# Token groups of an attention and two-MoE kernel: 512, 512, 512 and 768 tokens instead of 512, 512, 640 and 640

## The chip, the core and the metric

The kernel runs on one core of one Trainium2 chip. The metric is the device time of one execution in microseconds (us). The time before is 1117.15 us, the median of three runs (1117.76, 1117.15 and 1112.87).

## The reference

Four batches of 576 tokens, eight heads of 64 columns. Decayed causal attention gives 2304 rows of 512 columns, then come an RMS norm and two gated feed-forward layers, all in float32:

```python
def _moe_ref(x, w_gate, w_val, w_out, rms_g):
    rms = np.sqrt(np.mean(x * x, axis=-1, keepdims=True) + 1e-06)
    xn = x / rms * rms_g
    g = xn @ w_gate
    silu = g * (1.0 / (1.0 + np.exp(-g)))
    val = xn @ w_val
    return (silu * val @ w_out).astype(np.float32)
```

The second layer does the same without the norm. `w_gate` and `w_val` are 512 x 1536, `w_out` is 1536 x 512.

## The kernel before

**Groups.** Each batch's 576 tokens are cut into a block of 256 and a block of 320 (`QN`, L32). The four groups (`GROUPS`, L37) are the 256-blocks of batches 0 and 1, those of 2 and 3, the 320-blocks of 0 and 1, and the 320-blocks of 2 and 3. So the feed-forward layers run over 512, 512, 640 and 640 tokens. The attention of group g+1 runs in between the matmuls of group g: `attention` (L1481) starts each pair of heads when group g has done a given number of its 72 steps a layer pair (`steps`, `UNIT_SPREAD` L59; the last two entries belong to the last group).

**Matmuls.** A float32 operand is split into a high part in a 32-bit matmul format and the rest, and each product is three matmuls: high x high, high x low, low x high (`mm3`, L1668). Activations lie with the model dimension on the partitions, so a matmul's moving operand has as many columns as tokens. Weights come in 36 pieces of 128 x 512 a layer: 24 for gate and value, 12 for the output. A piece takes part in four tiles of 128 x 128, so a group of one matmul width has 2 layers x 36 pieces x 4 tiles x 3 = 864 matmuls. `moe` (L1682) goes over the groups. In groups 0 and 1 one thread works on both blocks at once, 512 columns a matmul. In group 2 the two blocks do not fit in 512, so two threads (`thread` 0 and 1) each do 320 columns with the same piece: 1728 matmuls of 320. Of these a third are output products, with `H` (and `late_h`) as moving operand; the rest have `X`.

**The last group** uses a seven-product scheme (`seven` L1371, `seven_out` L1261): a 2 x 2 block product with 7 instead of 8 products, its two column halves being the two 320-blocks. It has 1512 matmuls of 320 columns (L1388 to L1390 and L1306 to L1308). `right` (L1054) makes its moving operands (`b11`, `b21`, `b22`, `t1` to `t4`, for two row halves: 14 splits into high and low) from the normed attention output `xT`. `make_sums` (L1109) makes its weight sums ahead of time, during groups 1 and 2, paced by `S_AT` (L53): two pieces loaded, two results stored, for 36 units. `left` (L1148) and `out_left` (L1177) load them.

**Buffers.** Weight pieces live in eight 512 KB slots (`whl`), with three more (`XW`) once the attention is over; `XT32` adds five float32 load buffers, and `STS` five tiles for partial sums.

**Order.** All instructions are ordered at build time by a planner (`Plan`, L127): it gives each engine a cost function for each operation, lets generators wait for events and buffer slots, and issues what can start first. `either` picks among engines, with a handicap such as `HAND_LO`. All DMAs go out on one queue, SP, in the planned order. What the chip executes is this fixed order on each engine, with semaphores.

**Norm.** `norm` (L945) waits for a block's eight heads, sums squares, and scales. For groups 0 to 2 it writes a temporary that `split_x` (L1029) splits into `X`; for the last group it scales `xT` in place (L1011), and `right` takes it from there, block by block.

Of the kernel before, what the change touches and what calls it, by code (L numbers as in the profile page):

```python
# [8 lines left out]
F32 = mybir.dt.float32  # L9
# [21 lines left out]

QN = (SPLIT, S - SPLIT)  # L32
# [3 lines left out]
NMAX = max(QN)  # L36
GROUPS = ((0, (0, 1)), (0, (2, 3)), (1, (0, 1)), (1, (2, 3)))  # L37
# [16 lines left out]
XW, XT32, BSLOTS, STS = 3, 5, 3, 5  # L54
# [4 lines left out]
UNIT_SPREAD = ((0, 0), (0, 0), (-16, 1), (12, 5), (4, 4), (36, 4), (4, 4), (28, 4))  # L59
# [4 lines left out]
HAND_T = 0.0  # L64
HAND_CONV = (0, 0, 0, 0, 0)
# [192 lines left out]
def tile_attention_moe_moe(  # L258
# [76 lines left out]
    mb_slots = Slots(tiles(MB, [P, NMAX], F32, "mb"))  # L335
# [17 lines left out]
    zeros = HH[MT - 1][1][:, 1]  # L353
# [17 lines left out]
    rows = late_h.rearrange("p m i s n -> p (m i s n)")  # L371
    lent = [rows[:, 2 * i * WP : 2 * (i + 1) * WP].rearrange("p (t w) -> p t w", t=2) for i in range(LENT)]
# [95 lines left out]
    tt_here, out_p7, h_free, HQ = Event(), Event(), (Event(), Event()), []  # L468
# [7 lines left out]
    TT["t1"] = [[x[:, 1, :NMAX] for x in XX[c]] for c in range(2)]  # L476
# [154 lines left out]
    def pair_queries(hds, before, started, done):  # L631
# [97 lines left out]
        e = yield hi_op(n, xT[h // 2][s][:, :n], bank[:, :n], e, xT_free[hd.g][s], psum=True)  # L729
# [185 lines left out]
    def wide_values(hd, x, hl, ready, used_, done):  # L915
# [6 lines left out]
        def mm():  # L922
# [12 lines left out]
        to = xT[k][s][r0 : r0 + D, :n]  # L935
# [3 lines left out]
            "DVE", dve(n), lambda: nc.vector.tensor_tensor(to, bank[:D, :n], o[:D, :n], op=ALU.add), e, xT_free[hd.g][s]  # L939
# [5 lines left out]
    def norm(g, s, done):  # L945
# [3 lines left out]
        for k in range(KT):  # L949
            both = (done[2 * k], done[2 * k + 1])  # L950
            x = xT[k][s]
            if k == 0:
                e = yield op("ACT", act(n), lambda: nc.scalar.activation(acc[:, :n], x[:, :n], AF.Square), *both)
            else:
                sq, e0 = yield Take(tmp_slots, both)
                e1 = yield op("ACT", act(n), lambda: nc.scalar.activation(sq[:, :n], x[:, :n], AF.Square), e0, *both)
# [191 lines left out]
    def left(i):  # L1148
# [9 lines left out]
        for x, n, src, ready in (  # L1158
# [12 lines left out]
            spawn(load_split(n, t, o, src, ready, es[x], e0, e1), pr)  # L1171
# [37 lines left out]
    def load_split(n, t, o, src, ready, ev, *deps):  # L1209
# [7 lines left out]
        e = yield lo_op(n, lo, t[:, :n], hi, e, *deps)  # L1217
# [3 lines left out]
    def finish_pair(layer, m, s, bank, e, half, mid):  # L1221

        n = NMAX
        yield wait(mid, e, *h_free)
# [7 lines left out]
            "DVE", dve(n), lambda: nc.vector.tensor_tensor(o, th[:, :n], bank[:, :n], op=ALU.mult), e, mid, *h_free,  # L1232
# [28 lines left out]
    def seven_out(layer, g, at0):  # L1261

        n = NMAX
# [28 lines left out]
        for q, (p, x, off, name) in enumerate(OUT):  # L1292
# [30 lines left out]
            progress(g, at0, 0)  # L1323

    def combine(layer, d, bank, made):
        n = NMAX

        def out_(dd, s, b, a, *deps):
            if not layer:
                e = yield op("DVE", dve(n), lambda: nc.vector.tensor_tensor(xT[dd][s][:, :n], b[:, :n], a, op=ALU.add), *deps)  # L1330
# [4 lines left out]
            spawn(send(dd, s, z, e), 0.1)  # L1335
# [28 lines left out]
    def send(d, s, z, e):  # L1364
        kind, blocks = GROUPS[NG - 1]
        n = QN[kind]
        rows = out[d * P : (d + 1) * P].rearrange("p (b t) -> p b t", b=B)[:, blocks[s], QOFF[kind] : QOFF[kind] + n]
        e = yield op("SP", dma(P * 4 * n), lambda: nc.sync.dma_start(rows, z[:, :n]), e)
        tmp_slots.give(z, e)

    def seven(layer, base, m):  # L1371

        n = NMAX
# [4 lines left out]
        def rights(name):  # L1378
# [3 lines left out]
            return [[x[:, s, :n] for x in XX[k + c]] for c in range(2)]  # L1382
# [140 lines left out]
    def switch():  # L1523
# [375 lines left out]
```

## Time and profile before

| | us |
|---|---|
| runs | 1117.76, 1117.15, 1112.87 |
| median | 1117.15 |
| profiled execution, its own time | 1114.52 |
| its span, first to last instruction | 1112.7 |
| busy: TensorE matmuls / VectorE / ScalarE / GpSimd | 1092.0 / 808.4 / 631.0 / 474.5 |
| group 0 and 1, matmuls of 512 columns | 69.3 to 562.4 |
| group 2, matmuls of 320 columns, two threads | 562.5 to 886.3 |
| last group, seven products | 886.4 to 1109.3 |

PE is TensorE, DVE VectorE, ACT ScalarE, POOL GpSimd, SP the queue that issues DMAs. A matmul's listed duration is longer than its share of the engine, because matmuls overlap; the cost of one in a dense stretch is the distance between the starts of two neighbours. The two rows of a matmul line that differ only in columns are different forms. The share of the DMA engines is a mean over 16; it can read a little over 1.

### The profile page before, as it was taken

How to read it: one execution, taken by the hardware profiler on the slowest of the kernel's cores; microseconds unless marked ns; L12 is line 12 of the kernel's file. 1: busy time of each engine (PE TensorE's matmuls, PEld its weight loads, DVE VectorE, ACT ScalarE, POOL GpSimd, SP SyncE). 2: the span in 40 equal slices, each digit the busy share in tenths (PEclk: the TensorE clock that was granted, in tenths of full speed). 3: DMA queues.
4: the chain of work that ended last, by engine and by line, in shares of the span. 5: the costliest groups of instructions: out<-in, count | busy, mean ns of one | idle time of the engine just before them, and what ended most of it. 6: DMA issues, size and time to landing. Idle time of an engine off the chain costs nothing.

```text
span 1112.7 us, 19530 instructions
## 1 busy us (share of the span) xinstructions
PE 1092.0 (98%) x6411; PEld 999.2 (90%) x6411; DVE 808.4 (73%) x1774; ACT 631.0 (57%) x1462; POOL 474.5 (43%) x502
## 2 busy tenths in 40 slices
PE   8989999998999999999999999999999999999998
PEld 7968888886888888888899999999999999999998
DVE  6988888888557757667567766676766278878884
ACT  5967788886556655766434554455553343453442
POOL 1323202224156566656354555364455564124410
PEclk8999999998999999999999999999999999999999
DMA  7655788675999775875989798786778656975694
GB/s 223 218 181 191 252 274 298 220 227 161 332 378 325 244 244 205 280 247 200 317 277 354 267 319 309 267 270 235 253 268 291 214 196 216 295 266 190 206 300 139
DMA packets 135225, 282.35 MB, mean 254 GB/s; under 512 B 13906, under 2 KB 56210, under 8 KB 135122
## 3 DMA queue, kind: packets, MB, share of 16 engines
q1 hardware_dynamic: 135124, 281.10, 74.5%
q8 instruction: 51, 0.84, 0.3%
q14 instruction: 50, 0.41, 0.1%
HBM read 194.32 MB, written 86.65 MB: 253 GB/s over the span
## 4 chain that ended last, share of the span: by engine, by line
PE 83%; DVE 7%; DMA 6%; POOL 2%; issue 2%; SPq 1%; ACT 1%; POOLq 0%; ACTq 0%
PE bank L1671 17%; PE bank L1673 17%; PE bank L1672 17%; PE bank L1389 4%; PE bank L1390 4%; PE bank L1388 4%; PE bank L926 3%; PE bank L898 3%; DMA w<-w_f 2%; PE bank L1308 2%; PE bank L1307 2%; PE bank L1306 2%; PE bank L789 2%; PE bank L790 2%; DMA w<-w 1%
## 5 line engine op out<-in xcount | busy, mean ns | idle before, releaser
L1671 PE MATMUL bank<-X,whl 128*128 128x320 f32 (+1 forms) x756 | 270.7, 358 | 3.3 <-ACT X L287 3.3
L1672 PE MATMUL bank<-X,whl 128*128 128x320 f32 (+1 forms) x756 | 264.4, 350 | 0.8 <-POOL X L292 0.6
L1673 PE MATMUL bank<-X,whl 128*128 128x320 f32 (+1 forms) x756 | 264.4, 350 | 0.0
L292 POOL TENSOR_TENSOR whl<-w,whl 128x512 fp32r<-128x512 f32 x123 | 159.5, 1300 | 185.4 <-ACT whl L287 128.8
L1671 PEld LDWEIGHTS bank<-X,whl 128*128 128x128 f32 x756 | 142.4, 188 | 17.4 <-ACT X L287 3.6
L1673 PEld LDWEIGHTS bank<-X,whl 128*128 128x128 f32 x756 | 142.2, 188 | 15.1
L1672 PEld LDWEIGHTS bank<-X,whl 128*128 128x128 f32 x756 | 142.6, 189 | 14.5 <-POOL X L292 1.1
L287 ACT CAST whl<-w 128x512 fp32r<-128x512 f32 x169 | 104.3, 622 | 70.2 <-DMA w<-w_sums 24.4
L1671 PE MATMUL bank<-H,whl 128*128 128x512 f32 (+1 forms) x272 | 98.6, 362 | 4.4 <-ACT whl L287 4.4
L1673 PE MATMUL bank<-H,whl 128*128 128x512 f32 (+1 forms) x272 | 96.9, 356 | 0.2 <-DVE whl L292 0.2
L1672 PE MATMUL bank<-H,whl 128*128 128x512 f32 (+1 forms) x272 | 96.7, 355 | 0.0
L1775 ACT ACTIVATE tmp<-bank 128x512 f32<-128x512 f32 (+1 forms) x96 | 50.0, 521 | 56.2 <-PE bank L1673 56.0
L1778 DVE SCALAR_TENSOR_TENSOR tmp<-tmp,bank 128x512 f32<-128x512 f32 (+1 forms) x96 | 55.9, 583 | 31.3 <-ACT tmp L1775 31.0
L1800 DVE SCALAR_TENSOR_TENSOR bank<-tmp,bank 128x320 f32<-128x320 f32 (+1 forms) x84 | 48.7, 580 | 33.5 <-PE bank L1673 32.7
L1607 POOL TENSOR_SCALAR w<-w,rebase 128x512 f32<-128x512 f32 x24 | 24.2, 1010 | 105.5 <-DVE wk L1619 42.0
L807 DVE TENSOR_REDUCE tm<-bank 128x1 f32<-128x512 f32 (+1 forms) x96 | 51.1, 561 | 17.7 <-PE bank L796 12.3
L1671 PEld LDWEIGHTS bank<-H,whl 128*128 128x128 f32 x272 | 51.3, 188 | 10.9 <-ACT whl L287 4.9
L1613 ACT ACTIVATE w<-w,kbias 128x512 uint8<-128x512 uint8 x41 | 60.1, 1465 | 1.0 <-DVE w L1605 0.6
L1673 PEld LDWEIGHTS bank<-H,whl 128*128 128x128 f32 x272 | 51.2, 188 | 7.3 <-DVE whl L292 0.9
L1672 PEld LDWEIGHTS bank<-H,whl 128*128 128x128 f32 x272 | 51.3, 189 | 5.6
L1805 ACT CAST H<-bank 128x320 fp32r<-128x320 f32 (+1 forms) x64 | 32.0, 500 | 41.0 <-DVE bank L1800 39.9
L910 DVE TENSOR_TENSOR pl<-bank,ph 128x512 fp32r<-128x512 f32 (+1 forms) x80 | 49.7, 631 | 6.7 <-ACT ph L287 6.1
(267 smaller groups left out, 2925.2 us busy)
## 6 DMA issues: line engine op xcount, KB each, us to landing
whl<-w_split SPq DMA_DIRECT2D x85, 512.0 KB
w<-w SPq DMA_DIRECT2D x72, 512.0 KB
w<-w_f SPq DMA_DIRECT2D x144, 256.0 KB
w_split<-whl SPq DMA_DIRECT2D x72, 512.0 KB
w_f<-w SPq DMA_DIRECT2D x72, 256.0 KB
w_sums<-w SPq DMA_DIRECT2D x48, 256.0 KB
w_sums_split<-whl SPq DMA_DIRECT2D x23, 512.0 KB
raw<-qk SPq DMA_DIRECT2D x32, 288.0 KB
```

The costliest lines, as they stand in the source:

```text
L287: nc.scalar.copy(o, i)
L292: (nc.vector if e == "DVE" else nc.gpsimd).tensor_tensor(o, a, b, op=ALU.subtract)
L807: em = yield op("DVE", dve(m), lambda: nc.vector.tensor_reduce(st[:, c + i : c + i + 1], bank[:, :m], axis=AX.X, op=ALU.max), e)
L910: e = yield op("DVE", dve(n), lambda: nc.vector.tensor_tensor(low, src, o.bitcast(F32), op=ALU.subtract), e)
L1388: nc.tensor.matmul(o, w[:, 0, cs], xh, start=c == 0, stop=False)
L1613: lambda e: nc.scalar.activation(u8[:, :, 4], u8[:, :, 3], AF.Identity, scale=1.0 / 32, bias=kbias)
L1671: nc.tensor.matmul(o, wh[:, cs], xh, start=start, stop=False)
L1672: nc.tensor.matmul(o, wh[:, cs], xl, start=False, stop=False)
L1673: nc.tensor.matmul(o, wl[:, cs], xh, start=False, stop=stop)
L1775: e = yield op("ACT", actp(n), lambda: nc.scalar.activation(th[:, :n], bank[:, :n], AF.Tanh, scale=0.5), e, e0)
L1778: lambda: nc.vector.scalar_tensor_tensor(th[:, :n], th[:, :n], 1.0, bank[:, :n], op0=ALU.add, op1=ALU.mult), e,
L1800: lambda: nc.vector.scalar_tensor_tensor(o, th[:, :w], factor, bank[:, :w], op0=ALU.mult, op1=ALU.mult), e, mid,
```

## The change

The groups of tokens become 512, 512, 512 and 768. Group 2 takes the whole 320-block of batch 0 and the first 192 tokens of batch 1's; the last 128 tokens of batch 1's block are normed in place in `xT` and join the last group, whose halves are now 384 columns (`NL`). `moe` has one thread; every matmul of groups 0 to 2 has 512 columns (`NW`) and every one of the last group 384. `xT`, `X` and `H` lose their block dimension and become plain rows of columns. `join` lets the last group's operand preparation wait for both blocks' norms. Output tiles go out in one DMA per run of tokens (`tokens`). In the last group there is one extra float32 load buffer instead of five and two extra weight slots instead of three; four of the five partial-sum tiles are the norm's old tiles. The heads' pace (`UNIT_SPREAD`), a priority for the last group's first weights (`HEAD_PRIO`) and two engine handicaps (`HAND_LAST`) change. What the attention computes is the same, and so are all weights that are loaded. The diff, cut to its core:

```diff
+NW, NL = 512, 384
+COLS = ((0, 256), (0, 256), (128, 448), (0, 320))
+LEFT_OVER = COLS[2][0] + NW
+TOKENS = (
+    ((0, 0, 256), (1, 0, 256)),
+    ((2, 0, 256), (3, 0, 256)),
+    ((0, 256, 320), (1, 256, 192)),
+    ((2, 256, 320), (3, 256, 320), (1, 448, 128)),
+)
...
-XW, XT32, BSLOTS, STS = 3, 5, 3, 5
+XW, XT32, BSLOTS, STS = 2, 1, 3, 1
...
-UNIT_SPREAD = ((0, 0), (0, 0), (-16, 1), (12, 5), (4, 4), (36, 4), (4, 4), (28, 4))
+UNIT_SPREAD = ((0, 0), (0, 0), (-16, 1), (12, 5), (4, 4), (32, 4), (4, 3.5), (28, 3.5))
...
+HEAD_PRIO = 1.2
+HAND_LAST = (0.2, 0.2)
...
-    def lo_op(n, o, i, hi, *deps):
-        hand = HAND_LO[plan.phase]
+    def lo_op(n, o, i, hi, *deps, hand=None):
+        hand = HAND_LO[plan.phase] if hand is None else hand
...
-    mb_slots = Slots(tiles(MB, [P, NMAX], F32, "mb"))
+    mbs, accs = tiles(MB, [P, NL], F32, "mb"), tiles(2, [P, NL], F32, "acc")
...
-    accs = tiles(2, [P, NMAX], F32, "acc")
-    xT = [tiles(2, [P, NMAX], F32, f"xT{k}_") for k in range(KT)]
...
-    XX = [tiles(2, [P, 2, NMAX], F32R, f"X{k}_") for k in range(KT)]
-    HH = [tiles(2, [P, 2, NMAX], F32R, f"H{m}_", hp) for m in range(MT - 3)]
-
-    late_h = hp.tile([P, 3, 2, 2, NMAX], F32R, name="late_h")
...
+    xT = tiles(KT, [P, 2 * NL], F32, "xT")
+    XX = [tiles(2, [P, 2 * NL], F32R, f"X{k}_") for k in range(KT)]
+    HH = [tiles(2, [P, NW], F32R, f"H{m}_", hp) for m in range(MT - 3)]
+    late_h = hp.tile([P, 3, 2, NW], F32R, name="late_h")
     HH += [[late_h[:, m, i] for i in range(2)] for m in range(3)]
...
-    def view(t, s, n):
-        return t[:, :, :n] if s is None else t[:, s, :n]
-
-    def part(t, s, n):
-        return t[:, :n] if s is not None else t[:, : 2 * n].rearrange("p (s n) -> p s n", s=2)
+    def cols(t, g, s):
+        c = COLS[g][s]
+        return t[:, c : c + QN[GROUPS[g][0]]]
...
-        if g == NG - 1:
-            for k in range(KT):
-                x = xT[k][s][:, :n]
-                e = yield op(
-                    "DVL", dve(n),
-                    lambda: nc.vector.scalar_tensor_tensor(x, x, gam[:, k : k + 1], rb[:, :n], op0=ALU.mult, op1=ALU.mult),
-                    eb, gam_here,
-                )
-                later(last_x[0][k][s], e)
-            mb_slots.give(rb, e)
-            return
-        for k in range(KT):
-            xn, e0 = yield Take(tmp_slots, (x_free[g][s], gam_here))
+
+        at = n if g < NG - 2 else QN[1] - (COLS[2][1] + QN[1] - LEFT_OVER) * s if g == NG - 2 else 0
+        for k in range(KT if at else 0):
+            xn, e0 = yield Take(tmp_slots, (x_free[g], gam_here))
             e = yield op(
-                "DVL", dve(n),
+                "DVL", dve(at),
                 lambda: nc.vector.scalar_tensor_tensor(
-                    xn[:, :n], xT[k][s][:, :n], gam[:, k : k + 1], rb[:, :n], op0=ALU.mult, op1=ALU.mult
+                    xn[:, :at], cols(xT[k], g, s)[:, :at], gam[:, k : k + 1], rb[:, :at], op0=ALU.mult, op1=ALU.mult
                 ), eb, e0,
             )
-            spawn(split_x(g, s, k, xn, e), 1)
+            spawn(split_x(g, s, k, xn, at, e), 1)
+        for k in range(KT if at < n else 0):
+            x = cols(xT[k], g, s)[:, at:]
+            e = yield op(
+                "DVL", dve(n - at),
+                lambda: nc.vector.scalar_tensor_tensor(x, x, gam[:, k : k + 1], rb[:, at:n], op0=ALU.mult, op1=ALU.mult),
+                eb, gam_here,
+            )
+            later(in_place[k][s if g == NG - 1 else 2], e)
         mb_slots.give(rb, e)
-        later(xT_free[g + 1][s], e)
-
-    def split_x(g, s, k, xn, e):
-        n = QN[GROUPS[g][0]]
-        hi, lo = (view(x, s, n) for x in XX[k])
-        e = yield hi_op(n, hi[:, :n], xn[:, :n], e, x_free[g][s])
-        e = yield lo_op(n, lo[:, :n], xn[:, :n], hi[:, :n], e)
+        later(normed[g][s], e)
+
+    def split_x(g, s, k, xn, n, e):
+        c = COLS[g][s] - COLS[g][0]
+        hi, lo = (x[:, c : c + n] for x in XX[k])
+        e = yield hi_op(n, hi, xn[:, :n], e, x_free[g])
+        e = yield lo_op(n, lo, xn[:, :n], hi, e)
         tmp_slots.give(xn, e)
         later(x_ready[g][s][k], e)
+
+    def join(k):
+
+        for s in range(2):
+            yield wait(*in_place[k][s : s + 2], in_place[k][1])
+            later(last_x[0][k][s], Event(max(e.t for e in (*in_place[k][s : s + 2], in_place[k][1]))))
...
+        e = yield lo_op(n, lo, i, hi, e, *deps, hand=HAND_LAST[0])
...
-        n = NMAX
-        (b11, b12), (b21, b22) = xT[c], xT[c + 2]
+        n = NL
+        (b11, b12), (b21, b22) = ((xT[k][:, :n], xT[k][:, n:]) for k in (c, c + 2))
         (e11, e12), (e21, e22) = last_x[layer][c], last_x[layer][c + 2]
-        free = (x_free[NG - 1][0], x_free[NG - 1][1]) if layer == 0 else ()
+        free = (x_free[NG - 1],) if layer == 0 else ()
...
-            spawn(load_split(n, t, o, src, ready, es[x], e0, e1), pr)
+            spawn(load_split(n, t, o, src, ready, es[x], e0, e1), pr - HEAD_PRIO * (j % NPIECE < 2 * HEAD))
...
+        e = yield lo_op(n, lo, t[:, :n], hi, e, *deps, hand=HAND_LAST[1])
...
+    def send(d, z, tokens, e):
+        es = []
+        for c, b, q, n in tokens:
+            rows = out[d * P : (d + 1) * P, b * S + q : b * S + q + n]
+            es.append((yield op("SP", dma(P * 4 * n), lambda: nc.sync.dma_start(rows, z[:, c : c + n]), e)))
+        tmp_slots.give(z, Event(max(x.t for x in es)))
+    def tokens(g, start, n):
+        at = 0
+        for b, q, m in TOKENS[g]:
+            first, last = max(at, start), min(at + m, start + n)
+            if first < last:
+                yield first - start, b, q + first - at, last - first
+            at += m
...
+        yield wait(*normed[NG - 1])
+        for x in mbs + accs:
+            st_slots.add(x, max(e.t for e in normed[NG - 1]))
...
-    users = [(2 if GROUPS[i // FIRST][0] else 1) + (i // FIRST == 1) for i in range(TOTAL)]
+    users = [1 + (i // FIRST == 1) for i in range(TOTAL)]
...
-    def mm3(o, w, c, x, s, n, start, stop):
-        (xh, xl), cs = (view(t, s, n) for t in x), slice(c * P, (c + 1) * P)
+    def mm3(o, w, c, x, start, stop):
+        (xh, xl), cs = (t[:, :NW] for t in x), slice(c * P, (c + 1) * P)
...
-    def moe(thread):
-
+    def moe():
+
+        n = NW
         for g in range(NG):
-            kind, blocks = GROUPS[g]
-            s = thread if kind else None
-            if (not kind or g == NG - 1) and thread:
-                continue
-            mine = range(2) if s is None else (s,)
-            n = QN[kind]
-            width = n * len(mine)
             at = 0
-            ready = [[x_ready[g][i][k] for i in mine] for k in range(KT)]
+            ready = [[x_ready[g][i][k] for i in range(2)] for k in range(KT)]
...
-                                "PE", 3 * pe(width),
-                                lambda: mm3(o, w_tiles[pc], k, XX[k], s, n, k == 0, k == KT - 1),
+                                "PE", 3 * pe(n),
+                                lambda: mm3(bank, w_tiles[pc], k, XX[k], k == 0, k == KT - 1),
...
+    for k in range(KT):
+        spawn(join(k), 0)
+    spawn(moe(), 5)
```

## Rows read from the trace of the kernel before

**Rows 1.** The page's part 1, busy time; engine, us, share, instructions.
```profile
PE 1092.0 (98%) x6411; PEld 999.2 (90%) x6411; DVE 808.4 (73%) x1774; ACT 631.0 (57%) x1462; POOL 474.5 (43%) x502
```

**Rows 2.** Windows by stage: length, busy us (count), clock, DMA share, GB/s.
```profile
70.00:562.10 492.10, 487.34 (x2328) 406.17 (x2329) 362.17 (x724) 328.15 (x675) 203.97 (x207) 0.99 0.75 256
562.10:886.20 324.10, 321.93 (x2194) 316.05 (x2193) 213.99 (x503) 158.96 (x410) 174.81 (x197) 1.00 0.80 276
886.20:1112.70 226.50, 222.63 (x1515) 221.84 (x1513) 174.70 (x373) 95.57 (x219) 74.63 (x68) 1.00 0.68 226
```

**Rows 3.** Timeline of PE at its longest wait, and after it.
```profile
266.58 0.79 PE L1671 MATMUL bank<-H,whl 128*128 128x512 f32 x1 [4.42 <-ACT whl L287]
...
268.97 0.63 PE L1672 MATMUL bank<-late_h,whl 128*128 128x512 f32 x1
269.40 0.63 PE L1673 MATMUL bank<-late_h,whl 128*128 128x512 f32 x1
```

**Rows 4.** Timeline of PE, 320 columns: first and last of ten, starts first.
```profile
885.04 0.31 PE L1671 MATMUL bank<-late_h,whl 128*128 128x320 f32 x1
...
886.36 0.31 PE L1388 MATMUL bank<-X,xwhl 128*128 128x320 f32 x1
```

**Rows 5.** Timeline of PE, 512 columns: H, seven rows; X, thirteen rows.
```profile
259.43 0.40 PE L1672 MATMUL bank<-H,whl 128*128 128x512 f32 x1
...
260.83 0.40 PE L1672 MATMUL bank<-H,whl 128*128 128x512 f32 x1
...
501.18 0.39 PE L1673 MATMUL bank<-X,whl 128*128 128x512 f32 x1
...
503.90 0.39 PE L1673 MATMUL bank<-X,whl 128*128 128x512 f32 x1
```

**Rows 6.** Windows of L1671 alone, one of a product's three lines, group 2.
```profile
562.40:886.30 323.90, 181.52 (x576) 108.09 (x576) 1.00 0.80 276
```

**Rows 7.** Windows of L1388 alone, then L1306 alone, in the last group.
```profile
886.30:1112.70 226.40, 103.82 (x336) 62.98 (x336) 1.00 0.68 226
...
886.30:1112.70 226.40, 51.86 (x168) 31.53 (x168) 1.00 0.68 226
```

**Rows 8.** Timeline of PE: attention scores of 384 columns, two neighbours.
```profile
333.28 0.33 PE L790 MATMUL bank<-kb,qb 68*128 68x384 f32 x1
333.46 0.23 PE L796 MATMUL bank<-mir 128*128 128x128 f32 x1
```

**Rows 9.** Timeline at the end: DMA issues, last matmul, last sum.
```profile
1107.24 2.97 SPq L1368 DMA_DIRECT2D zT<-tmp  x2
...
1109.02 0.30 PE L1308 MATMUL bank<-h11h,whl 128*128 128x320 f32 x1
1109.36 0.49 DVE L1334 TENSOR_TENSOR tmp<-bank,st 128x320 f32<-128x320 f32 x1 [2.14 <-PE bank L1308]
```

**Rows 10.** DVE rows by form in group 2: count, busy us, mean ns.
```profile
L1800 DVE SCALAR_TENSOR_TENSOR bank<-tmp,bank 128x320 f32<-128x320 f32 x48 | 23.7, 494 | 12.9 <-PE bank L1673 12.1
L910 DVE TENSOR_TENSOR pl<-bank,ph 128x512 fp32r<-128x512 f32 x24 | 16.5, 686 | 1.9 <-ACT ph L287 1.5
```

**Rows 11.** DMA packets of group 2's window, 562 to 886 us.
```profile
DMA packets 38090, 89.55 MB, mean 276 GB/s; under 512 B 4271, under 2 KB 10318, under 8 KB 38057
```

**Rows 12.** Windows of a long full DMA stretch and of group 2's first third.
```profile
278.20:361.60 83.40, 83.40 (x390) 69.44 (x389) 50.55 (x91) 48.73 (x99) 36.77 (x44) 1.00 0.95 345
562.40:660.00 97.60, 96.97 (x662) 95.51 (x662) 69.17 (x160) 50.97 (x132) 58.73 (x68) 1.00 0.86 300
```

**Rows 13.** Timeline: early operand splits, the norm scales, last split.
```profile
848.18 1.72 POOL L292 TENSOR_TENSOR X<-xT,X 128x320 fp32r<-128x320 f32 x2
...
856.42 0.87 POOL L292 TENSOR_TENSOR X<-xT,X 128x320 fp32r<-128x320 f32 x1
...
858.26 1.01 DVE L1011 SCALAR_TENSOR_TENSOR xT<-xT,gam,mb 128x320 f32<-128x320 f32 x2
...
870.50 0.88 POOL L292 TENSOR_TENSOR t<-st,t 128x320 fp32r<-128x320 f32 x1
```

More of the change, by code (lines that the diff above doesn't have):

```diff
@@ L370, in tile_attention_moe_moe @@
     w_slots = Slots(tiles(WSLOTS, [P, 2, WP], F32R, "whl"))
-    rows = late_h.rearrange("p m i s n -> p (m i s n)")
-    lent = [rows[:, 2 * i * WP : 2 * (i + 1) * WP].rearrange("p (t w) -> p t w", t=2) for i in range(LENT)]
+    lent = [late_h[:, i] for i in range(LENT)]
     for x in lent:
@@ L475, in tile_attention_moe_moe @@
     TT = {}
-    TT["t1"] = [[x[:, 1, :NMAX] for x in XX[c]] for c in range(2)]
+    TT["t1"] = [[x[:, NL:] for x in XX[c]] for c in range(2)]
     lefts = {}
@@ L1221, in finish_pair @@
     def finish_pair(layer, m, s, bank, e, half, mid):
-        n = NMAX
-        yield wait(mid, e, *h_free)
+        n = NL
+        yield wait(mid, e, h_free)
         up, r = m % 4 // 2, 2 * (m // 4) + m % 2
@@ L1244, in pair_sums @@
     def pair_sums(layer, r):
-        n, ev = NMAX, hid[layer][r]
-        yield wait(*h_free)
+        n, ev = NL, hid[layer][r]
+        yield wait(h_free)
         f11, b12, b21, b22, t2, t4 = (HQ[r][1][x] for x in ("t1", "t3", "b21", "b22", "t2", "t4"))
@@ L1334, in out_ @@
             e = yield op("DVE", dve(n), lambda: nc.vector.tensor_tensor(z[:, :n], b[:, :n], a, op=ALU.add), e0, *deps)
-            spawn(send(dd, s, z, e), 0.1)
+            spawn(send(dd, z, list(tokens(NG - 1, s * n, n)), e), 0.1)
             return e
@@ L1362, in combine @@
         st_slots.give(a, e)
-    def send(d, s, z, e):
-        kind, blocks = GROUPS[NG - 1]
-        n = QN[kind]
-        rows = out[d * P : (d + 1) * P].rearrange("p (b t) -> p b t", b=B)[:, blocks[s], QOFF[kind] : QOFF[kind] + n]
-        e = yield op("SP", dma(P * 4 * n), lambda: nc.sync.dma_start(rows, z[:, :n]), e)
-        tmp_slots.give(z, e)
+    def send(d, z, tokens, e):
[11 more added lines that the diff above has]
+            at += m
     def seven(layer, base, m):
-        n = NMAX
+        n = NL
         u = lefts[base + 2 * m]
@@ L1381, in rights @@
             k, s = XB[name]
-            return [[x[:, s, :n] for x in XX[k + c]] for c in range(2)]
+            return [[x[:, s * n : (s + 1) * n] for x in XX[k + c]] for c in range(2)]
         def product(o, l, off, name):
@@ L1541, in switch @@
             if name not in TT:
-                TT[name] = [[tp.tile([P, NMAX], F32R, name=f"{name}{c}{i}") for i in range(2)] for c in range(2)]
+                TT[name] = [[tp.tile([P, NL], F32R, name=f"{name}{c}{i}") for i in range(2)] for c in range(2)]
         for i in range(XT32):
@@ L1549, in switch @@
         for i in range(STS):
-            st_slots.add(tp.tile([P, NMAX], F32, name=f"st{i}"), now)
+            st_slots.add(tp.tile([P, NL], F32, name=f"st{i}"), now)
         later(tt_here, Event(now))
+        yield wait(*normed[NG - 1])
+        for x in mbs + accs:
+            st_slots.add(x, max(e.t for e in normed[NG - 1]))
     def switch_hidden():
-        yield wait(*h_free)
+        yield wait(h_free)
         hidden.close()
@@ L1558, in switch_hidden @@
         for r in range(len(PAIRS)):
-            parts_ = tuple(hq.tile([P, NMAX], F32R, name=f"h11{x}_{r}") for x in "hl")
-            t = {x: hq.tile([P, NMAX], F32, name=f"h{x}_{r}") for x in ("t1", "t2", "t3", "t4", "b21", "b22")}
+            parts_ = tuple(hq.tile([P, NL], F32R, name=f"h11{x}_{r}") for x in "hl")
+            t = {x: hq.tile([P, NL], F32, name=f"h{x}_{r}") for x in ("t1", "t2", "t3", "t4", "b21", "b22")}
             HQ.append((parts_, t))
@@ L1737, in moe @@
                             half = []
-                            spawn(gate(width, bank, e, half, mid), 0.0)
+                            spawn(gate(bank, e, half, mid), 0.0)
                         else:
-                            spawn(finish(s, n, pair, half, mid, HH[m], h_ready[m], H_PSUM[g](2 * m + thread), 0.5), 0.0)
-                    progress(g, at, thread)
-                if layer and g + 1 < NG:
-                    for i in mine:
-                        later(x_free[g + 1][i], e)
+                            spawn(finish(pair, half, mid, HH[m], h_ready[m], H_PSUM[g](2 * m)), 0.0)
+                    progress(g, at)
+                if layer:
+                    later(x_free[g + 1], e)
                 y_ready = [Event() for _ in range(KT)]
@@ L1747, in moe @@
                     bank, e0 = yield Take(banks, (h_ready[0],))
-                    o = part(bank, s, n)
                     for j in range(3):
@@ L1789, in gate_silu, with finish @@
         later(mid, e)
-    def finish(s, n, pair, half, mid, hl, ready, psum, factor):
+    def finish(pair, half, mid, hl, ready, psum):
+        n = NW
         bank, e = pair[1]
@@ L1809, in finish, with evac @@
             banks.give(bank, e)
-            e = yield hi_op(w, hi, o, e)
-            e = yield lo_op(w, lo, o, hi, e)
+            e = yield hi_op(n, hi, o, e)
+            e = yield lo_op(n, lo, o, hi, e)
             tmp_slots.give(th, e)
         later(ready, e)
-    def evac(s, n, bank, e, layer, d, g, ready):
-        w = n if s is not None else 2 * n
-        o = part(bank, s, n)
+    def evac(bank, e, layer, d, g, ready):
+        n = NW
         if layer == 0:
-            hi, lo = (view(x, s, n) for x in XX[d])
-            e = yield op("ACT", actp(w), lambda: nc.scalar.copy(hi, o), e)
-            e = yield op("DVE", dve(w), lambda: sub("DVE", lo, o, hi.bitcast(F32)), e)
+            hi, lo = (x[:, :n] for x in XX[d])
+            e = yield op("ACT", actp(n), lambda: nc.scalar.copy(hi, bank), e)
+            e = yield op("DVE", dve(n), lambda: sub("DVE", lo, bank, hi.bitcast(F32)), e)
             banks.give(bank, e)
@@ L1825, in evac @@
             z, e0 = yield Take(tmp_slots, ())
-            e = yield op("ACT", actp(w), lambda: nc.scalar.copy(z[:, :w], bank[:, :w]), e, e0)
+            e = yield op("ACT", actp(n), lambda: nc.scalar.copy(z, bank), e, e0)
             banks.give(bank, e)
-            kind, blocks = GROUPS[g]
-            rows = out[d * P : (d + 1) * P].rearrange("p (b t) -> p b t", b=B)[:, :, QOFF[kind] : QOFF[kind] + n]
-            rows = rows[:, blocks[0] : blocks[1] + 1] if s is None else rows[:, blocks[s]]
-            e = yield op("SP", dma(P * 4 * w), lambda: nc.sync.dma_start(rows, part(z, s, n)), e)
-            tmp_slots.give(z, e)
-    for s in range(2):
-        xT_free[0][s].t = 0.0
-        x_free[0][s].t = 0.0
+            spawn(send(d, z, list(tokens(g, 0, n)), e), 0.1)
+    x_free[0].t = 0.0
     spawn(decay(0, Event(2.6), Event(0.0)), 0)
@@ L1850, in tile_attention_moe_moe @@
     spawn(fill_stop(), 0)
-    for s in range(2):
-        spawn(moe(s), 5 + 0.0005 * s)
+    for k in range(KT):
+        spawn(join(k), 0)
+    spawn(moe(), 5)
     plan.run()
```

84 lines of the change are left out of this document (38 added, 46 removed).

## The prediction, made before the change was run

> **What bounds the kernel now.** I read the busy times first: TensorE's matmuls cover 1092.0 us of a span of 1112.7, and VectorE, the next, 808.4 [rows 1]. A share over the whole span can hide idle stages, so the windows by stage come next: from 70 us on, PE is busy in 487.3 of 492.1, 321.9 of 324.1 and 222.6 of 226.5 us, at a granted clock of 0.99 to 1.00 [rows 2]. In the list of waits the longest of PE is 4.4 us, for a weight split; the timeline shows it [rows 3]. So the kernel is a chain of matmuls that hardly waits, and what the change is worth is what it does to the cost of that chain, as long as the other engines and the DMAs still keep up.
>
> The cost of a matmul in a dense stretch is the distance between starts. At 320 columns nine distances take 1.32 us, 146.7 ns each [rows 4]. At 512 columns twelve distances take 2.72 us (226.7 ns) where the moving operand is X, and six take 1.40 us (233.3 ns) where it is H [rows 5]. At 2.4 GHz, 320 and 512 columns alone are 133.3 and 213.3 ns, so a matmul costs its columns and 13.3 ns more, with H at 512 columns 20 ns.
>
> **The sum, part by part.**
>
> *Group 2.* L1671 runs 576 times in it [rows 6], three lines make 1728 matmuls, all of 320 columns: 1728 x 146.7 ns = 253.5 us. The rest of the 323.9 us is attention. In their place come 864 of 512 columns, 576 with X and 288 with H: 576 x 226.7 + 288 x 233.3 ns = 197.8 us. That is 55.7 us less, although 110,592 columns less are only 46.1 us: the rest is the fixed cost of 864 matmuls.
>
> *Last group.* 336 + 168 matmuls on each of three lines [rows 7], 1512 in all, go from 320 to 384 columns. By the rows at 320, 64 columns more cost 26.7 ns: 40.3 us more. The trace has few matmuls of 384; one in the attention is followed after 180 ns [rows 8], against 173.3 by this sum. That bounds the term: at most 1512 x 33.3 ns = 50.4 us. I take 40.3, as the 320-column rows are of the same lines and operands.
>
> *H as a plain tile.* H and X lose a stride in groups 0 to 2. Should it be the stride that makes H 6.7 ns dearer, 864 matmuls gain 5.8 us; should X go the other way, 1728 matmuls lose 11.5. At 320 columns H costs no more than others [rows 4], which speaks for some gain, but rows of the same lines at 512 are nearest, and I take zero.
>
> *DMA.* All weights, sums and attention inputs are loaded as before. Output tiles go from 24 DMAs to 40, since each now leaves by runs of tokens: 16 more issues on SP. Two of them at the end take 2.97 us with the wait in between [rows 9], so one is at most 1.5 us, 24 us in all over the span. Weights are fetched several pieces of 2.7 us ahead of the matmuls that hide this; without that cover a weight would come 1.5 us late at each. Only the last tile's second issue shows: with a VectorE sum of 384 instead of 320 columns (0.49 us now), about 0.4 us more at the end.
>
> *The other engines* in group 2 have less time for the same attention. For the layers, 160 VectorE operations of 320 columns at 0.494 us become 80 of 512 at 0.686 [rows 10]: 24 us less, so 190 of 268 us, 71% after 66%. GpSimd's 174.8 us become 65% of the stage. Both are covered by the matmuls; if the cover goes, the splits of weights on GpSimd are late next, and PE waits for them as at 262 us. The extra norm operations on 128 tokens are four of a fraction of a us, far ahead of their use.
>
> *Buffers.* A step of the last group takes three of the large weight slots and 42 matmuls. Eleven slots at 6.16 us a step look 22.6 us ahead, ten at 7.28 us 24.3, so the smaller number costs nothing. The four norm tiles come free only after the last norm, which the operand splits wait for anyhow.
>
> The sum is -55.7 + 40.3 + 0.4 = **-15.0 us**. Against the profiled execution's own 1114.52 us it gives 1099.5; the median of the runs lies 2.6 us higher, which gives 1102.1. I forecast **1101**.
>
> A rule speaks against half of this. The Trainium skill, "TensorE: Matmul & The Clock Gate", section "Back-to-back issue gap", states an isolated gap of columns / 2.4 + 2.5 ns at full clock. By it group 2 would gain 48.2 us and the sum would be about -7.5. The trace disagrees with it, with 146.7 ns at 320 columns where the rule gives 135.8.
>
> **Rivals.**
>
> *Group 2 becomes bound by DMA: slower than before.* Its window moves 89.55 MB [rows 11] at a DMA share of 0.80 [rows 2]. In 268.2 us (323.9 - 55.7) the same bytes need 334 GB/s. If the DMAs bring R, the stage takes 89.55 MB / R: at 316 GB/s it is 283 us and the whole gain is gone, below 310 the kernel is slower by more than 0.5%. Group 2's own first third runs at 300 GB/s and a share of 0.86 [rows 12]; were that all that this mix of loads and stores allows, the stage would take 298.5 us and the kernel 1131. Against it: 83 us of the trace run at 345 GB/s, at a share of 0.95, with PE busy in 83.40 of 83.40 us [rows 12]. And the bytes needn't all fall there: the sums for the second layer can slip into the last group, which runs at 0.68 [rows 2]. So a partial loss of a few us is more likely than a full one.
>
> *The last group's operands come late.* Now the norm scales from 858.3 and the last operand split ends at 871.4 [rows 13], 15 us ahead of the group's first matmul at 886.36 [rows 4]. Three of the 14 splits have run before the scaling [rows 13], since one block's operands don't wait for the other's. With halves of 384 columns that mix both blocks all 14 wait. The 13.1 us for 11 splits grow to 13.1 x 14/11 x 1.2 = 20 us. The heads' last gate opens at step 52 instead of 56, and 19 pieces of 2.72 (X) or 2.80 us (H) then follow instead of 15 of 3.52: 52.6 us against 52.8, so the time from that gate to the end of the group stays. Of the 28.1 us from 858.3 to 886.36, 20 are needed and 8 are spare. If attention slips by more, PE waits. The trace prices a wait of 4.42 us [rows 3]: after it 512-column matmuls are 430 ns apart, the lower clock level, 1.2 GHz, for a few us, some 2 us more. Such a wait gives 1107.
>
> *Only the columns count.* If the 13.3 ns were not per matmul, the change would save its 13,824 columns (110,592 - 96,768), 5.8 us: 1111. The distances at both widths speak plainly against it. (The overhead that the Trainium skill's rule states would put the kernel in between, at 1109.)
>
> *The change doesn't do what it says.* That the last group's widths or counts differ from my reading can be seen in the counts below; I give it no chance of its own.
>
> **How the numbers follow.** About 0.5% (5.6 us: 1111.6 to 1122.7) is what a measurement of this kernel can tell from no change. The sum holds, with everything covered: 0.70, 1094 to 1107 with the bounds of H and of 384 columns and a wait like that at 262 us more or less. DMA-bound: 0.15, of which 0.04 still faster, 0.05 the same, 0.06 slower. Operands late: 0.12, of which 0.08 faster, 0.03 the same, 0.01 slower. Columns only: 0.03, 0.02 faster and 0.01 the same. With 0.69 and 0.01 from the first case: faster 0.83, same 0.10, slower 0.07. The range 1094 to 1111 leaves out the slower cases, part of the unchanged ones and a larger gain from H.
>
> **What would show it.** Right: group 2 has 864 matmuls some 227 to 233 ns apart and is 268 us long at a DMA share near 0.95; the last group has 1512, 173 ns apart, and takes about 266 us from its first matmul to the end; PE's waits stay under 10 us in sum. Wrong: matmuls at 180 ns in the last group (+10 us); waits of PE on weight splits in group 2 with half-clock matmuls behind them; a wait for X or t operands where the last group starts; or a group 0 or 1 whose length moves by more than 5 us.

## The result and the profile after

The changed kernel takes 1098.82 us, the median of four runs (1097.81 to 1101.38), against 1117.45 us for the kernel before beside it (1112.87 to 1118.11): a ratio of 0.9845, 95% interval [0.9814, 0.9877], 18.6 us less. The profiled execution takes 1098.85 us with a span of 1097.1; the one before took 1114.52 and 1112.7, so the two profiles lie 15.7 us apart.

The page's part 1 of the changed kernel, to set beside [rows 1]:

```profile
PE 1078.0 (98%) x5547; PEld 949.6 (87%) x5547; DVE 803.8 (73%) x1709; ACT 628.6 (57%) x1409; POOL 468.2 (43%) x492
```

Its windows by stage, with the columns of [rows 2]: groups 0 and 1, group 2, the last group and the end.

```profile
71.00:564.70 493.70, 488.97 (x2330) 407.49 (x2331) 359.20 (x729) 331.20 (x688) 215.84 (x218) 0.99 0.74 254
564.70:830.90 266.20, 265.79 (x1330) 223.82 (x1329) 189.14 (x429) 144.04 (x352) 153.54 (x180) 1.00 0.93 337
830.90:1097.10 266.20, 262.49 (x1513) 262.17 (x1511) 198.24 (x381) 105.88 (x214) 77.65 (x64) 1.00 0.60 194
```

PE is as full as before. Group 2 shrank from 323.9 to 266.1 us (its PE busy falls short of the stage by 0.4 us, before by 2.2) and the last group with the end grew from 226.5 to 266.2. The DMA share of group 2 rose from 0.80 to 0.93, that of the last group fell from 0.68 to 0.60. The four longest waits of PE over the whole span (in total, times, longest):

```profile
PE bank L1700 <- ACT whl L301: 4.4, 1, 4.4
PE bank L1700 <- ACT X L301: 3.3, 1, 3.3
PE bank L381 <- DVE H L368: 3.3, 1, 3.3
PE bank L658 <- DMA qk<-cum: 1.7, 1, 1.7
```

The first is the wait of [rows 3], untouched; none of the four lies in group 2 or the last group. Counts of one line each: L1700 in group 2, then L1414 and L1322 (the former L1388 and L1306) in the last group, as in [rows 6, 7].

```profile
564.73:830.85 266.12, 116.60 (x288) 54.00 (x287) 1.00 0.93 337
...
830.85:1093.30 262.45, 112.32 (x336) 62.91 (x335) 1.00 0.60 196
...
830.85:1093.30 262.45, 56.40 (x168) 31.59 (x168) 1.00 0.60 196
```

The distances between starts, in the timeline of PE: X at 512 columns (first and last of thirteen rows), H at 512 (of seven), then the last group's 384 (of seven).

```profile
572.91 0.39 PE L1700 MATMUL bank<-X,whl 128*128 128x512 f32 x1
...
575.63 0.39 PE L1700 MATMUL bank<-X,whl 128*128 128x512 f32 x1
...
829.22 0.40 PE L1702 MATMUL bank<-late_h,whl 128*128 128x512 f32 x1
...
830.62 0.40 PE L1702 MATMUL bank<-late_h,whl 128*128 128x512 f32 x1
830.85 0.34 PE L1414 MATMUL bank<-X,whl 128*128 128x384 f32 x1
...
831.89 0.33 PE L1414 MATMUL bank<-X,xwhl 128*128 128x384 f32 x1
```

Twelve distances take 2.72 us (226.7 ns), six take 1.40 us (233.3 ns), six take 1.04 us (173.3 ns). The DMA packets of group 2 and the windows of its two halves:

```profile
DMA packets 38285, 89.63 MB, mean 337 GB/s; under 512 B 4322, under 2 KB 10242, under 8 KB 38260
...
564.73:697.70 132.97, 132.97 (x668) 112.55 (x667) 87.16 (x199) 71.45 (x175) 74.16 (x88) 1.00 0.97 355
697.70:830.85 133.15, 132.74 (x663) 111.22 (x662) 101.90 (x231) 72.59 (x178) 79.38 (x92) 1.00 0.89 319
```

Nearly the same bytes as before [rows 11] in 58 us less. The first half runs at 355 GB/s with PE busy in every one of its 132.97 us. The timeline ahead of the last group: the first scores of the last pair of heads, the norm's scaling, the last operand split.

```profile
782.11 0.33 PE L802 MATMUL bank<-k,q 128*128 128x384 f32 x1
...
811.09 1.01 DVE L1034 SCALAR_TENSOR_TENSOR xT<-xT,gam,mb 128x320 f32<-128x320 f32 x2
...
828.95 0.55 DVE L306 TENSOR_TENSOR t<-acc,t 128x384 fp32r<-128x384 f32 x1
```

The last split ends at 829.50, 1.35 us ahead of the group's first matmul at 830.85; before, that was 15 us [rows 4, 13]. The end, as in [rows 9]:

```profile
1081.95 12.86 SPq L1385 DMA_DIRECT2D zT<-tmp  x12
...
1093.05 0.34 PE L1324 MATMUL bank<-h11h,whl 128*128 128x384 f32 x1
...
1093.43 0.56 DVE L1350 TENSOR_TENSOR tmp<-bank,acc 128x384 f32<-128x384 f32 x1 [2.56 <-PE bank L1324]
```

The span ends at 1097.1, 4.05 us after the last matmul's start, before 3.68.

### The profile page after: what moved, and what is told of

It is laid out like the page before. It is cut to its first block, busy times and chain, and to the rows that moved or that the text cites. A ratio compares the mean times of both kernels' runs of the same rounds, so it can differ in the third digit from the quotient of the medians.

```text
span 1097.1 us, 17688 instructions
## 1 busy us (share of the span) xinstructions
PE 1078.0 (98%) x5547; PEld 949.6 (87%) x5547; DVE 803.8 (73%) x1709; ACT 628.6 (57%) x1409; POOL 468.2 (43%) x492
## 4 chain that ended last, share of the span: by engine, by line
PE 90%; DVE 5%; DMA 2%; POOL 1%; issue 1%; ACT 0%; SPq 0%; POOLq 0%; ACTq 0%
PE bank L1700 18%; PE bank L1702 17%; PE bank L1701 17%; PE bank L1414 5%; PE bank L1416 5%; PE bank L1415 5%; PE bank L939 3%; PE bank L911 3%; PE bank L1324 3%; PE bank L1323 3%; PE bank L1322 3%; PE bank L802 2%; PE bank L803 2%; DMA w<-w 1%; PE bank L658 1%; PE bank L734 1%
## 5 line engine op out<-in xcount | busy, mean ns | idle before, releaser
L1700 PE MATMUL bank<-X,whl 128*128 128x512 f32 x564 | 227.5, 403 | 3.3 <-ACT X L301 3.3
L1702 PE MATMUL bank<-X,whl 128*128 128x512 f32 x564 | 221.0, 392 | 0.0
L1701 PE MATMUL bank<-X,whl 128*128 128x512 f32 x564 | 221.0, 392 | 0.0
L1700 PEld LDWEIGHTS bank<-X,whl 128*128 128x128 f32 x564 | 106.6, 189 | 23.8 <-ACT X L301 3.5
L1702 PEld LDWEIGHTS bank<-X,whl 128*128 128x128 f32 x564 | 106.3, 189 | 23.1
L1701 PEld LDWEIGHTS bank<-X,whl 128*128 128x128 f32 x564 | 106.6, 189 | 19.6 <-DVE X L306 0.4
L1700 PE MATMUL bank<-H,whl 128*128 128x512 f32 x215 | 87.4, 407 | 4.4 <-ACT whl L301 4.4
L1702 PE MATMUL bank<-H,whl 128*128 128x512 f32 x215 | 85.4, 397 | 0.2 <-DVE whl L306 0.2
L1701 PE MATMUL bank<-H,whl 128*128 128x512 f32 x215 | 85.2, 396 | 0.0
L1804 ACT ACTIVATE tmp<-bank 128x384 f32<-128x384 f32 x48 | 23.6, 491 | 90.8 <-DVE bank L1452 90.5
L1794 ACT ACTIVATE tmp<-bank 128x512 f32<-128x512 f32 x72 | 43.3, 601 | 40.6 <-PE bank L1702 39.1
L1796 DVE SCALAR_TENSOR_TENSOR tmp<-tmp,bank 128x512 f32<-128x512 f32 x72 | 49.2, 684 | 22.7 <-ACT tmp L1794 22.0
L306 DVE TENSOR_TENSOR whl<-w,whl 128x512 fp32r<-128x512 f32 x71 | 49.5, 702 | 20.9 <-ACT whl L301 20.6
L1817 DVE SCALAR_TENSOR_TENSOR bank<-tmp,bank 128x512 f32<-128x512 f32 x60 | 41.6, 694 | 26.6 <-PE bank L1702 25.9
L306 POOL TENSOR_TENSOR kb<-raw,k 64x576 fp32r<-64x576 f32 x31 | 44.3, 1429 | 20.2 <-ACT k L301 14.2
L1700 PEld LDWEIGHTS bank<-H,whl 128*128 128x128 f32 x215 | 40.6, 189 | 13.5 <-ACT whl L301 4.9
```

The source lines that it names most:

```text
L306: (nc.vector if e == "DVE" else nc.gpsimd).tensor_tensor(o, a, b, op=ALU.subtract)
L1700: nc.tensor.matmul(o, wh[:, cs], xh, start=start, stop=False)
L1701: nc.tensor.matmul(o, wh[:, cs], xl, start=False, stop=False)
L1702: nc.tensor.matmul(o, wl[:, cs], xh, start=False, stop=stop)
L1796: "DVE", dve(n), lambda: nc.vector.scalar_tensor_tensor(th, th, 1.0, bank, op0=ALU.add, op1=ALU.mult), e,
```

## The experiments

All times are medians; ratios are to the kernel before, run beside them. No experiment leaves out a part of the computation; the extra DMAs of some move data that nothing reads.

### Is the cost per matmul, or per column?

e1_halves does each 512-column matmul of group 2 as two of 256:

```diff
-        nc.tensor.matmul(o, wh[:, cs], xh, start=start, stop=False)
...
+        for i in range(halves):
+            t = slice(i * NW // halves, (i + 1) * NW // halves)
+            nc.tensor.matmul(o[:, t], wh[:, cs], xh[:, t], start=start and i == 0, stop=False)
```

> The changed kernel, with each 512-column matmul of group 2 done as two of 256 columns on the same weights: 1728 matmuls, the columns and the DMAs as they are. Theory (a matmul costs its columns and 13.3 ns): 1728 x 120 ns is 207.4 us against 197.8, so group 2 grows by 9.6 to 11.5 us, from 266 to about 276, and the kernel comes to about 1109. Rival (only the columns count): group 2 stays at 266 us and the kernel at 1099.

Measured: 1110.95 us, ratio 0.9952 [0.9932, 0.9973]. Its group 2 in the windows view, first and last of 17 rows of the timeline of PE, and its largest wait there:

```profile
562.83:843.40 280.57, 275.89 (x2193) 270.47 (x2192) 191.09 (x434) 140.09 (x348) 147.98 (x171) 0.99 0.90 317
...
563.06 0.28 PE L1704 MATMUL bank<-X,whl 128*128 128x256 f32 x1
...
564.98 0.28 PE L1702 MATMUL bank<-X,whl 128*128 128x256 f32 x1
...
PE bank L911 <- POOL dA L861: 2.6, 3, 1.6
```

Sixteen distances take 1.92 us: 120 ns, 256 / 2.4 and 13.3. Group 2 is 14.5 us longer. Its PE busy falls 4.7 us short of the stage, mostly a wait for the heads, against 0.4; without these 4.3 us it is 10.2 us, inside the 9.6 to 11.5 expected. "Only the columns count" is excluded. Each half loads its weights again (2192 weight loads in PEld, 1329 in the changed kernel), so the 13.3 ns belong to a matmul with its weight load; the two are not told apart here. With H as moving operand 256 columns cost less than with X, first and last of 25 rows:

```profile
820.69 0.28 PE L1702 MATMUL bank<-H,xwhl 128*128 128x256 f32 x1
...
823.53 0.28 PE L1702 MATMUL bank<-H,xwhl 128*128 128x256 f32 x1
```

Twenty-four distances take 2.84 us, 118.3 ns each. So H's extra cost at 512 columns is not a fixed one.

### How near is the DMA bound?

e2_copy1 and e3_copy2 add one or two DMAs of 256 KB from memory to memory behind the loads of each unit of sums, hidden from the planner, so that the order of all instructions stays:

```diff
+        def load_more():
+            nc.sync.dma_start(tv, w_d[j2])
+            nc.sync.dma_start(EXTRA[unit, 0], w_d[j])
...
-        el = yield op("SP", dma(P * WP * 4), lambda: nc.sync.dma_start(tv, w_d[j2]), e0, stored[j2])
+        el = yield op("SP", dma(P * WP * 4), load_more, e0, stored[j], stored[j2])
```

> The changed kernel in the same order, with one more DMA of 256 KB (memory to memory) beside the loads of each unit of weight sums: about 8 MB more in group 2, 98 MB. Rival of the prediction, now as a theory (the DMAs carry about 345 to 350 GB/s and group 2 at 337 is just below the bound): 98 MB take 280 us or more, so group 2 grows by 14 us or more, PE waits on weights, and half-clock matmuls follow. Other theory (there is room to nearly 390 GB/s, as single windows of 13 us show): 98 MB in 266 us are 367 GB/s, PE waits under 3 us in sum, the kernel within 4 us of 1099.

> As e2_copy1 with two such DMAs a unit: about 106 MB in group 2. Bound at 345 to 350 GB/s: group 2 takes 303 us or more, 37 us more than now, and the kernel 1136 or more. Room to 390 GB/s: 272 us, the kernel about 1106. This run also reads the limit itself: the rate in group 2 when PE waits for it.

Measured: 1116.43 us (ratio 0.9994 [0.9976, 1.0013]) and 1134.01 us (1.016 [1.0111, 1.021]). Group 2 of e2_copy1 in the windows view and its two largest waits of PE there, then the same of e3_copy2:

```profile
566.19:849.90 283.71, 270.60 (x1330) 224.71 (x1329) 189.90 (x425) 143.48 (x352) 153.40 (x180) 0.99 0.95 345
...
PE bank L911 <- POOL dA L861: 5.5, 4, 1.9
PE bank L939 <- DVE ph L923: 2.1, 2, 1.2
```

```profile
565.53:867.40 301.87, 279.49 (x1329) 231.44 (x1328) 187.93 (x421) 142.41 (x351) 153.53 (x180) 0.96 0.96 350
...
PE bank L911 <- POOL dA L861: 7.2, 3, 2.9
PE bank L802 <- POOL q L306: 4.9, 3, 2.2
```

Group 2 grows by 17.6 and 35.8 us, the size that a bound at 345 to 350 GB/s forecast: the rates are 345 and 350, at shares of 0.95 and 0.96. By 350 GB/s the changed kernel's 89.63 MB would take 256 us, so its group 2 would stand some 10 us, 4%, from such a bound (an estimate). That the DMAs carry no more is not shown, as another stretch of the changed kernel, in groups 0 and 1, runs faster with PE busy throughout:

```profile
301.70:356.60 54.90, 54.90 (x258) 45.85 (x257) 31.05 (x57) 31.87 (x71) 34.05 (x32) 1.00 1.00 378
```

One detail was wrong: PE does not wait for weights but for the heads of the next group, whose transposes (L911) stand in PE's fixed order and whose inputs come late.

e8_before_copy1 and e9_before_copy2 put the same DMAs, equally hidden, into the kernel before; e10_late_copy1 puts one into the changed kernel with later sums (e7_sums_late below).

> The kernel before, with the same extra DMA of 256 KB a unit of sums as in e2_copy1. Theory (the DMAs carry 345 to 350 GB/s, and only a stage that needs more grows): 98 MB in group 2's 324 us are 301 GB/s, PE waits no more than now, the kernel within 3 us of 1116. Rival (the extra DMAs cost by standing in the SP queue, about 17 us as in e2_copy1, whatever the rate): 1133.

> The kernel before with two extra DMAs a unit. Theory: 106 MB in 324 us are 326 GB/s, still under 345: at most 4 us longer, 1120. Rival (queue): about 35 us as in e3_copy2, 1151.

> The changed kernel with the sums paced as in e7_sums_late and one extra DMA a unit as in e2_copy1. Theory (rate alone): some 87 MB in group 2's 267 us are 326 GB/s, so the 17 us of e2_copy1 shrink to under 4 and the kernel is near 1102. Rival (queue): 1115 or more.

Measured: 1123.86 us (1.0077 [1.0047, 1.0106]), 1133.86 us (1.0156 [1.012, 1.0191]) and 1108.11 us (0.992 [0.9894, 0.9947]). Neither theory holds: each time is between the two. Group 2 of e8_before_copy1 (6.0 us longer than before), then of e10_late_copy1 (4.5 us longer than e7_sums_late's), in the windows view:

```profile
566.17:896.06 329.89, 323.59 (x2193) 317.44 (x2192) 210.81 (x502) 158.24 (x410) 175.24 (x197) 0.99 0.85 296
```

```profile
566.48:840.20 273.72, 268.65 (x1329) 224.42 (x1328) 184.94 (x422) 136.03 (x341) 121.71 (x145) 0.99 0.91 320
```

Group 2 of e9_before_copy2 in two windows, and its two largest waits of PE over both:

```profile
563.07:683.00 119.93, 111.67 (x747) 108.03 (x745) 75.43 (x183) 55.47 (x145) 65.10 (x75) 0.99 0.96 343
683.00:907.46 224.46, 217.89 (x1447) 214.11 (x1447) 133.34 (x319) 102.38 (x266) 109.46 (x123) 0.96 0.83 288
...
PE bank L898 <- POOL dA L848: 9.6, 5, 3.1
PE bank L898 <- ACT dA L846: 3.0, 2, 1.8
```

The stage of e9_before_copy2 grows by 20.5 us at a mean of 307 GB/s, far under 345. Its first 120 us run at a share of 0.96. Over the whole stage PE waits 12.6 us on the heads' tiles, 4.6 of them in the first window, and the granted clock is 0.99 and 0.96 in the two windows. But the first half of the changed kernel's group 2 runs at 355 GB/s with no wait at all. So a mean rate under 345 GB/s is not enough, and a full queue is not harmful as such. A new theory: what costs is loads that land later than the fixed order expects. e11_planned_copy2 is e9_before_copy2 with the extra DMAs told to the planner:

```diff
+        for x in range(2):
+            yield op("SP", dma(P * WP * 4), lambda: nc.sync.dma_start(EXTRA[unit, x], w_d[j2 if x else j]), e0, stored[j], stored[j2])
```

> The kernel before with the same two extra DMAs a unit as e9_before_copy2 (20 us longer in group 2), but now told to the planner, so that the order of the instructions allows for them. Theory (the extra bytes cost because loads land later than the fixed order expects, not because the DMAs can't carry them: 106 MB in 324 us are 326 GB/s): the growth of group 2 shrinks from 20 to under 8 us, and PE's waits on the heads shrink with it. Rival (the bytes cost 20 us wherever they stand): group 2 stays near 344 us and the kernel near 1134.

Measured: 1114.05 us, ratio 0.997 [0.9948, 0.9992]. Group 2 in the windows view, and all waits of PE in it:

```profile
566.46:886.77 320.31, 320.10 (x2193) 315.92 (x2192) 202.79 (x498) 156.66 (x409) 172.79 (x200) 1.00 0.92 331
...
PE bank L898 <- DVE tmp L1781: 0.2, 1, 0.2
```

The same extra bytes, 16 MB in group 2, cost nothing: 320.3 us at 331 GB/s against 323.9, PE idle for 0.2. So in the kernel before the plan was the cause, that is the order of the instructions and the place of the loads in it, not the bytes. For the changed kernel with extra DMAs in the plan this was not tried, so how much of the 17.6 and 35.8 us is a limit of the DMAs and how much a plan that did not know of them stays open; 106 MB in 266 us would be 398 GB/s, above every rate seen over a stage.

### What makes the last heads late?

e5_gate_late and e6_gate_early move the gate of the last block's heads by four steps; e7_sums_late spreads the sums:

```diff
-UNIT_SPREAD = ((0, 0), (0, 0), (-16, 1), (12, 5), (4, 4), (32, 4), (4, 3.5), (28, 3.5))
+UNIT_SPREAD = ((0, 0), (0, 0), (-16, 1), (12, 5), (4, 4), (32, 4), (4, 3.5), (32, 3.5))
...
+UNIT_SPREAD = ((0, 0), (0, 0), (-16, 1), (12, 5), (4, 4), (32, 4), (4, 3.5), (24, 3.5))
...
-S_AT = (60, 2)
+S_AT = (60, 2.6)
```

> The changed kernel with the last block's heads gated four steps later (32 + 3.5 h instead of 28 + 3.5 h). Theory A (the gate sets when the last heads start): they start some 14 us later, the operand splits end about 13 us after the last group should start, PE waits 5 to 13 us there at half clock after it, and the kernel is 6 to 15 us longer. Theory B (the heads' loads and splits set it, not the gate, since the DMA queue is full): their start moves by less than 4 us and the time by less than 3.

> The changed kernel with the last block's heads gated four steps earlier (24 + 3.5 h). Theory A (the gate sets the start): the last norm's scaling moves from 811 to about 797 us, the operand splits have some 15 us to spare, and the time stays within 1.5 us of 1099, as nothing waited there. Theory B (loads and splits set it): the scaling stays within 4 us of 811, and the time too stays.

> The changed kernel with the weight sums paced every 2.6 steps instead of 2, so that some 8 of the 36 units fall into the last group. DMA share in group 2 falls from 0.93 to about 0.80 and the last group's rises. If the full DMA queue is what makes the last heads late, the last norm's scaling comes several us before 811 us; if not, it stays. Either way PE did not wait, so the time stays within 2 us of 1099; if the sums then come late for the last group, PE waits in its second half and the kernel is longer.

Measured: 1099.68, 1100.41 and 1100.40 us (ratios 0.9844, 0.9853 and 0.9852, each within 0.0045 at 95%), the same as the change. The last heads' first scores and the norm's scaling in the timeline of e5_gate_late, then of e6_gate_early:

```profile
783.10 0.33 PE L802 MATMUL bank<-k,q 128*128 128x384 f32 x1
...
813.04 1.02 DVE L1034 SCALAR_TENSOR_TENSOR xT<-xT,gam,mb 128x320 f32<-128x320 f32 x2
```

```profile
783.53 0.33 PE L802 MATMUL bank<-k,q 128*128 128x384 f32 x1
...
812.52 1.01 DVE L1034 SCALAR_TENSOR_TENSOR xT<-xT,gam,mb 128x320 f32<-128x320 f32 x2
```

Later or earlier gate, the heads start at 783.1 and 783.5 us and the norm scales at 813.0 and 812.5 (782.1 and 811.1 in the change): theory B, the gate does not set it. e7_sums_late, its group 2 in the windows view, the norm's scaling and the last operand split:

```profile
563.29:832.50 269.21, 266.07 (x1329) 223.40 (x1328) 183.70 (x422) 136.59 (x341) 121.66 (x145) 1.00 0.87 301
...
802.34 1.01 DVE L1034 SCALAR_TENSOR_TENSOR xT<-xT,gam,mb 128x320 f32<-128x320 f32 x2
...
815.91 0.55 DVE L306 TENSOR_TENSOR t<-acc,t 128x384 fp32r<-128x384 f32 x1
```

With the DMA share at 0.87 instead of 0.93 (about 0.80 was expected), the norm scales at 802.3, and the last split ends at 816.5, 16 us ahead of the last group at 832.5. So the weight sums, not the gate, make the last heads late. Whether their DMAs do it or their work on the engines is not shown: pacing the sums more slowly takes both out of group 2, and GpSimd's busy time there falls from 153.5 to 121.7 us. The changed kernel's trace shows both on the way of the last head. There is one `raw` buffer for the loads of these heads; the load is issued at 769.42, as the splits of the head before end, and the first split of the new head follows at 776.12, 6 us ahead of the scores:

```profile
769.42 0.60 SPq L608 DMA_DIRECT2D raw<-qk  x1
...
776.12 0.66 ACT L301 CAST k<-raw 128x576 fp32r<-128x576 f32 x1
```

Nothing waited for the late heads in the change, and the time stays; in group 2 of e7_sums_late PE waits 3.1 us for heads. No version here beats the change.

### The handicaps and the priority

e4_nohand sets `HAND_LAST = (None, None)` and `HEAD_PRIO = 0`.

> The changed kernel without the two new handicaps and the priority (HAND_LAST and HEAD_PRIO undone), so that the planner gives the last group's low parts to GpSimd again. Theory (the heads now end so late that the operand splits have only 1 to 2 us to spare): the splits end after the last group should start, PE waits 2 to 6 us there, and the kernel is 2 to 9 us longer. Rival (these parts do nothing, as the prediction costed them): no wait there, the time within 1.5 us of 1099.

Measured: 1102.95 us, ratio 0.9886 [0.9847, 0.9925], whose interval overlaps the change's. The largest wait of PE from 800 us on, and the last operand split, on GpSimd now:

```profile
PE bank L1416 <- DVE whl L306: 1.2, 1, 1.2
...
829.79 1.04 POOL L306 TENSOR_TENSOR t<-acc,t 128x384 fp32r<-128x384 f32 x1
```

The last split ends at 830.83, 0.8 us ahead of the group's start at 831.6: the forecast wait of 2 to 6 us there did not come. PE waits 1.2 us at 967 us, for a weight split. That these parts are worth 4 us is possible by the medians, not shown.

## Why the prediction was right

*The sum.* Forecast -15.0 us, measured -15.7 between the profiled executions. Group 2: -55.7 forecast, 323.89 to 266.12 us, -57.8 measured; the 2 us more are PE's idle time there, 2.2 us before and 0.4 after, which the sum had left as it was. Last group: +40.3 forecast; from first to last matmul 222.66 to 262.20 us, +39.5. End: +0.4 forecast, +0.37. Groups 0 and 1: 493.2 to 493.7 us, as forecast unchanged, but they start at 71.1 instead of 69.3; that belongs to no step, and group 2's start lies between 562.5 and 566.5 over all these kernels. The medians, 18.6 us apart against the 16 that 1101 stood for, differ from this because the profiled execution of before lies 2.9 us under its median.

*The unknown sizes.* 384 columns cost 173.3 ns, not the 180 that bounded them. H as a plain tile still costs 233.3 ns: the stride was not the cause, and taking zero was right. The cost per matmul was tested by halving (e1_halves); 864 matmuls fewer at 13.3 ns are 11.5 us, the larger part of the gain. The Trainium skill's 2.5 ns a matmul ("TensorE: Matmul & The Clock Gate", "Back-to-back issue gap"), which that section gives for an isolated matmul and not for a stream with weight loads, is not what this stream shows: 13.3 ns at 256, 320, 384 and 512 columns with X. One reading was wrong, without an effect on the sum: the wait at 262 us is put down to weight splits on GpSimd, while its row names ScalarE [rows 3].

*The slower rival.* Its rate was met: group 2 ran at 337 GB/s where 334 were forecast, and e2_copy1 shows that 8 MB more, unplanned, give 17.6 us back. What it had wrong is where PE would wait (the heads, not weights) and that a mean rate decides: e9_before_copy2 loses 20.5 us at 307 GB/s, e11_planned_copy2 none at 331. The argument that 83 us at 345 GB/s pass with PE busy held.

*The step that failed.* "The time from that gate to the end of the group stays", hence 8 us to spare for the operand splits. Measured: 1.35 us. The last heads' first scores begin 48.7 us ahead of the last group (782.11 to 830.85), in the trace of before 62.8 (823.53 to 886.36), and four steps' shift of the gate was to keep that; the gate did not set it (e5_gate_late, e6_gate_early), but the weight sums in the stage did (e7_sums_late), by their DMAs or their engine work. The splits themselves took 18.4 us from the norm's scaling, forecast 20. It cost nothing because 1.35 us are enough; that so much was left is luck, as the prediction's 8 us were not there.

## What to carry to other kernels

Where PE never waits, a change is priced by the distances between starts of the very shapes it removes and adds, with the fixed cost of each matmul apart from its columns: here 13,824 columns fewer are only 5.8 us, while 864 matmuls fewer are 11.5, of which H's dearer 512 columns take 1.9 back. Then ask of the shortened stage what its unchanged bytes now need in GB/s, and look for a stretch of the same trace that sustains it. With a fixed order of instructions the mean rate is only half the answer: loads must land when the order expects them, so extra traffic belongs in the plan (e9_before_copy2 and e11_planned_copy2 show it for the kernel before).

## What the runs showed of the hardware

In a dense stretch a matmul of this kernel costs 233.3 ns at 512 columns with H as moving operand and 226.7 with X, stride or no stride; at 320 columns [rows 4] and at 384 no such difference shows, and at 256 it turns round, 118.3 with H and 120 with X (e1_halves). Its cause stays open. DMA rates over whole stages reach 350 GB/s (e3_copy2); in the changed kernel they are 355 over 133 us and 378 over 55 us, with PE busy throughout.
